# A mixture-of-experts kernel: the first search compares in three parts and is counted column by column, the first layer is cut at 256 tokens, and candidates are counted by a turning sum in all quarters

## The chip, the cores and the metric

The kernel runs on one core of a Trainium2 chip. The metric is the device time of one execution in microseconds, as the median of several runs. The core has engines that run side by side and wait for each other by semaphores: TensorE (PE in the profile; PEld are its weight loads), VectorE (DVE), ScalarE (ACT), GpSimd (POOL), and SyncE (SP), which here only issues transfers. VectorE's 128 lanes are the partitions; a quarter, or quadrant, is 32 of them.

## The reference

The program is an attention block followed by a layer of eight experts. Cut to what matters:

```python
kv = np.einsum('bhsd,bhse->bhde', k, v)                  # batch 8, heads 8, seq 576, head_dim 64
out = np.einsum('bhsd,bhde->bhse', q, kv)
rms = np.sqrt(np.mean(out * out, axis=-1, keepdims=True) + 1e-06)
x = (out / rms * g_norm)                                 # then reshaped to N = 4608 tokens of D = 512

cap = N // E                                             # 576 tokens for each of E = 8 experts
logits = x @ w_gate
for idx in np.argsort(-logits.flatten()):                # best pairs first
    tok, e = idx // E, idx % E
    if assigned[tok] >= 0 or counts[e] >= cap: continue
    assigned[tok] = e; counts[e] += 1
for e in range(E):                                       # w1: 512 x 1024, w2: 1024 x 512
    h = np.maximum(x[assigned == e] @ w1[e], 0.0)
    out[assigned == e] = h @ w2[e]
```

The greedy assignment fills the experts one after another. The kernel finds, for each round, the score at which the next expert becomes full, by a search over thresholds.

## The kernel before

**Attention** (to about 137 us) makes the tokens, writes them to `x_dram`, and leaves the logits in `lg`, laid out as 128 partitions by 36 columns (`GC`) for each expert. While it runs, `early` (line 280) already makes the first comparison of the first search for the columns that are ready.

**A search** is `threshold(t, over)` (line 493), for rounds t = 0 to 6. It has seven steps (`NSTEP`). In each step 32 candidate thresholds (`NCAND`) lie between two ends. `compare` (line 265) writes `over`: for each partition, column and candidate, whether the token's best score `mx` reaches the candidate, 36 x 32 = 1152 elements a partition. TensorE counts them by expert (line 503): nine matmuls, each with four columns of `over` (4 x 32 = 128) as weights and the same four columns of `best` as moving data. A product of 128 rows thus holds four column groups, of which only the blocks on the diagonal are wanted. VectorE subtracts three of these from `goal` (line 509, `need`), and compares the last with what remains (line 513, `full`; `n_full` counts the experts that are filled at a candidate). From the number of candidates with `n_full` above a half it derives the new ends.

For t = 0 that number is made by a matmul with ones (line 529, `k_ps`), and `pick_end` (line 521) reads the ends from a list. For t > 0 it is made on VectorE: line 543 spreads the flags in a 32 x 64 block, line 544 turns it in 32 x 32 blocks, line 545 sums it to `kk`, and line 549, once for each quarter of the partitions, multiplies `kk` by a width and adds the old lower end. Small values of these steps lie in one PSUM tile (`held_ps`), as named pieces.

After the seven steps, `assign` (line 560) settles which tokens the round takes and which expert it was; `fetch` (line 657) loads that expert's weights, works out the list of its tokens and gathers them from `x_dram` in five blocks of 128, the last of 64 (line 707, on GpSimd). `turn` (line 771) transposes each block on TensorE (line 783), and ScalarE copies it to `xt` with a factor (line 786). `warm` (line 652) gives TensorE matmuls without use[...].

**An expert's layers** are `layers(t)` (line 797). The first layer runs over two halves of the tokens, c = 0 and c = 1, of 288 columns each (`HALF`), and in each half over eight units of 128 hidden columns: four matmuls of 128 x 288 a unit (line 832; each appears as two records in the trace), then a ReLU on ScalarE (line 835). The second layer is a product of 2 x 2 blocks in seven multiplications instead of eight (line 881); block height is `TH` = 256 tokens, and GpSimd makes the sums of blocks (lines 813 and 823). The remaining 64 tokens follow at line 892.

**The order of the work** is written out by hand for TensorE, VectorE and ScalarE (`manual_schedule`, line 903). For the first expert, search, fetch and the turning of three of the five blocks are emitted first, then the first layer. From then on the layers of expert t are generated matmul by matmul, and each yields a cost. Searches for later rounds are a second generator that yields a due time: how much of TensorE's work is to lie before its next piece is emitted. A step of a search is due 4.6 us after the last one (line 498), the costs being 0.487 for a matmul of the first layer (line 834) and 0.38 for one of the second. So the count of a step stands in TensorE's queue behind about ten matmuls of a first layer, and in the meantime VectorE makes the next comparison. The blocks of the next expert's tokens are turned at places in the layers that yield `None`: two in the second layer (`turns`, line 873), one at line 896, and two inside the next first layer (the `yield 0` at line 837).

Of the kernel before, what the change touches and what calls it, by code (L numbers as in the profile page):

```python
# [7 lines left out]
FT = mybir.dt.float32  # L8
# [17 lines left out]
def kernel(  # L26
# [251 lines left out]
    over0 = asg.tile([P, GC, NCAND], BF, name="over", tag="over", bufs=2)  # L278

    def early(c0, c1):  # L280
        choose(c0, c1)
        compare(over0, cand0, c0, c1)
# [176 lines left out]
    for nm, shape in (("step", (2, NCAND + 3)), ("cut", (2, GC)), ("mx", (GC,)), ("code_mx", (GC,)), ("mine", (GC,)),  # L459
                      ("shut", (E,)), ("code", (E,)), ("some", (2 * QP,)), ("some_t", (2, QP + 1)),  # L460
# [18 lines left out]
    nc.vector.memset(small_ps["some_t"][0:QP, 0, QP:QP + 1], 1.0)  # L479
    nc.vector.memset(small_ps["some_t"][0:QP, 1, QP:QP + 1], 0.0)  # L480
# [12 lines left out]
    def threshold(t, over):  # L493
# [3 lines left out]
        for s in range(NSTEP):  # L497
            yield 4.6 if s > 0 else 0.4 if first else 2.0 if t == 1 else 2.4
# [3 lines left out]
            for c in range(0, GC, G):  # L502
                nc.tensor.matmul(n_ps, lhsT=over[:, c:c + G].rearrange("p c n -> p (c n)"),  # L503
                                 rhs=best[:, :, c:c + G],
                                 start=(c == 0), stop=(c == GC - G))
            need = goal[0:QP]
            for g in range(1, G):
# [7 lines left out]
            if s + 1 < NSTEP:  # L515
                over = asg.tile([P, GC, NCAND], BF, name="over", tag="over", bufs=2)
            if first:
# [13 lines left out]
                if s + 1 < NSTEP:  # L531
                    cand_next = small("cand", NCAND + 2)
                    compare(over, candidates(s + 1, lo, cand_next[:, 0:NCAND + 1]))
# [4 lines left out]
            else:  # L538
# [3 lines left out]
                some, some_t, kk = (small_ps[k][0:QP] for k in ("some", "some_t", "kk"))  # L542
                nc.vector.tensor_scalar(some, in0=n_full.to_broadcast([QP, 2 * QP]), scalar1=0.5, scalar2=None, op0=AL.is_gt)
                nc.vector.transpose(some_t[:, :, 0:QP], some.rearrange("p (t n) -> p t n", t=2))
                nc.vector.reduce_sum(out=kk, in_=some_t, axis=AXX)

                lo_was, (ends, cand_ps) = lo, pieces()
                for g in range(G):
                    nc.vector.tensor_scalar(ends[g * QP:(g + 1) * QP], in0=kk, scalar1=width[0:QP, s:s + 1],  # L549
                                            scalar2=lo_was[0:QP], op0=AL.mult, op1=AL.add)  # L550
# [202 lines left out]
    def control(t):  # L753
# [13 lines left out]
        if t + 1 < E - 1:  # L767
            compared[t + 1] = asg.tile([P, GC, NCAND], BF, name="over", tag="over", bufs=2)
            compare(compared[t + 1], candidates(0, bottom, pieces()[1]))

    def turn(t):
# [3 lines left out]
        if t == 0:  # L775
# [205 lines left out]
```

## Time and profile before

Three runs took 705.28, 705.42 and 708.66 us; the median is 705.42. The profiled execution has a span of 700.7 us.

| Stretch of the profile | us | TensorE busy | VectorE busy |
|---|---|---|---|
| attention | 0 to 137 | 88.93 | 77.58 |
| first search, before its result is used | 137 to 163 | 3.95 | 21.17 |
| assignment, list, weights, tokens, first turns | 163 to 179.2 | 9.62 | 13.54 |
| first expert | 179.2 to 244.9 | 65.44 | 52.48 |
| second to fifth expert | 244.9 to 506.8 | 260.37 | 219.06 |
| sixth expert | 506.8 to 568.8 | 62.00 | 13.72 |

A line of the timeline gives the start in us, the duration, the engine, the line of the kernel, the operation, what it writes and reads with the shapes (partitions x elements), how many instructions are merged, and in brackets how long the engine was idle before it and which instruction ended that. Matmul ends are modelled, so a busy TensorE is one that has matmuls in flight.

### The profile page before, as it was taken

The page shows a single profiled execution, that of the slowest core. Times are in us where ns is not written, and L with a number is a line of the kernel's source. Part 1 is how long each engine was busy: PE and PEld are TensorE (multiplying, and loading weights), DVE is VectorE, ACT ScalarE, POOL GpSimd, SP SyncE. Part 2 cuts the span into 40 slices and gives each one's busy share as a digit, 9 for nine tenths or more (in the row PEclk, how much of TensorE's full clock was granted, in tenths as well). Part 3 has the DMA queues.
Part 4 walks back from the last instruction along what each step waited for, and adds up shares of the span by engine and source line. Part 5 has one row for each costly group of instructions (what it writes and reads, how often), then busy time and mean ns, then how long its engine had stood idle before and what let it go on. Part 6 is the DMA issues. An engine that isn't in the chain of part 4 may idle for free.

```text
span 700.7 us, 13351 instructions
## 1 busy us (share of the span) xinstructions
PE 612.3 (87%) x5370; PEld 477.0 (68%) x5370; DVE 412.0 (59%) x1368; ACT 165.2 (24%) x355; POOL 288.7 (41%) x271
## 2 busy tenths in 40 slices
PE   3777686314999999999999999999999999999994
PEld 2566575211678677867786788678778867877782
DVE  4344666888678978888888888878650130010011
ACT  1454564710221122022102111211121022112100
POOL 0135433201263563535615651753284165426422
PEclk9998978555999999999999999999999999999997
DMA  8987797214501800810801610630371252010001
GB/s 284 320 288 262 256 347 284 92 46 144 164 1 51 301 25 3 306 60 8 307 2 68 246 64 15 232 130 1 107 252 59 79 187 69 1 54 14 0 1 67
DMA packets 41405, 91.05 MB, mean 130 GB/s; under 512 B 3456, under 2 KB 3456, under 8 KB 41344
## 3 DMA queue, kind: packets, MB, share of 16 engines
q1 hardware_dynamic: 34752, 71.31, 29.1%
q0 software_dynamic: 5888, 18.88, 7.8%
q8 instruction: 42, 0.69, 0.4%
q14 instruction: 19, 0.16, 0.1%
q10 hardware_dynamic: 704, 0.02, 0.1%
HBM read 71.32 MB, written 18.87 MB: 129 GB/s over the span
## 4 chain that ended last, share of the span: by engine, by line
PE 79%; DVE 10%; issue 4%; DMA 2%; ACT 2%; POOL 1%; POOLq 0%; ACTq 0%; DVEq 0%; SPq 0%
PE h_ps L832 34%; PE y_ps L881 27%; PE y_ps L892 4%; PE o_ps L372 3%; PE qt_ps L301 3%; PE t_ps L783 3%; PE kv_ps L313 2%; PE given_ps L503 2%; DVE over L266 1%; DMA gw<-in_moe_w_gate_dram 1%; DVE kv L321 1%; DMA w_sb<-in_moe_w_dram 1%; DVE ms L380 1%; PE w_ps L340 1%; ACT sq L378 1%
## 5 line engine op out<-in xcount | busy, mean ns | idle before, releaser
L832 PE MATMUL h_ps<-xt,w_sb 128*128 128x288 f32 x1024 | 261.8, 410 | 0.8 <-ACT xt L786 0.8
L832 PEld LDWEIGHTS h_ps<-xt,w_sb 128*128 128x128 f32 x1024 | 189.8, 190 | 54.9 <-issue 5.7
L835 ACT ACTIVATE hid<-h_ps 128x288 f32<-128x288 f32 x128 | 52.5, 410 | 207.0 <-PE h_ps L832 197.9
L881 PE MATMUL y_ps<-tw,sh 128*128 128x256 f32 x384 | 87.3, 381 | 0.0
L852 DVE TENSOR_TENSOR y_sb<-y_ps,u 128x512 f32<-128x512 f32 x24 | 16.5, 689 | 113.8 <-PE y_ps L881 113.3
L881 PEld LDWEIGHTS y_ps<-tw,sh 128*128 128x128 f32 x384 | 71.7, 190 | 9.1
L823 POOL TENSOR_TENSOR sh<-hid 128x512 f32<-128x512 f32 x32 | 40.6, 1268 | 86.4 <-ACT hid L835 86.4
L707 POOL DMA_INDIRECT xg<-x_dram,ids x40 | 38.1, 953 | 68.5 <-DMA w_sb<-in_moe_w_dram 42.7
L786 ACT ACTIVATE xt<-t_ps,g_col 128x512 f32<-128x512 f32 (+1 forms) x40 | 25.8, 644 | 144.9 <-PE t_ps L783 112.0
L881 PE MATMUL y_ps<-w_sb,hid 128*128 128x256 f32 x256 | 58.3, 382 | 0.0
L266 DVE TENSOR_TENSOR over<-mx,held_ps 128x1152 bf16<-128x1152 f32 x42 | 56.8, 1353 | 1.5
L881 PEld LDWEIGHTS y_ps<-w_sb,hid 128*128 128x128 f32 x256 | 48.0, 190 | 6.6
L859 POOL TENSOR_TENSOR y_sb<-u,u 128x512 f32<-128x512 f32 x8 | 10.2, 1270 | 96.2 <-DVE u L852 96.2
L399 POOL TENSOR_TENSOR xo<-o_sb,inv 128x512 f32<-128x512 f32 x31 | 32.5, 1078 | 34.6 <-ACT sq L378 17.3
L790 POOL DMA_INDIRECT out_dram<-y_sb,outs x32 | 31.3, 977 | 37.1 <-issue 21.2
L813 POOL TENSOR_TENSOR tw<-w_sb 128x512 f32<-128x512 f32 x32 | 39.9, 1269 | 12.1 <-DMA w_sb<-in_moe_w_dram 11.9
L549 DVE TENSOR_SCALAR held_ps<-held_ps,width 32x2 f32<-32x2 f32 x144 | 41.3, 287 | 5.3
L503 PEld LDWEIGHTS <-over 128*128 128x128 bf16 x441 | 17.6, 97 | 38.2 <-DVE over L266 27.3
L372 PE MATMUL o_ps<-kvx,qt 64*64 64x72 f32 x1152 | 31.0, 251 | 9.5 <-issue 8.8
L503 PE MATMUL given_ps<-best,over 128*128 128x32 bf16 x441 | 19.3, 179 | 21.4 <-DVE over L266 19.2
L372 PEld LDWEIGHTS o_ps<-kvx,qt 64*64 64x64 f32 x1152 | 25.3, 153 | 15.1 <-issue 13.6
L380 DVE TENSOR_REDUCE ms<-sq 128x8 f32<-128x512 f32 x36 | 24.0, 679 | 17.9 <-ACT sq L378 17.8
(210 smaller groups left out, 827.4 us busy)
## 6 DMA issues: line engine op xcount, KB each, us to landing
w_sb<-in_moe_w_dram SPq DMA_DIRECT2D x16, 1024.0 KB, 6.8
w_sb<-in_moe_w_dram SPq DMA_DIRECT2D x8, 2048.0 KB, 15.7
k_sb<-in_k_dram SPq DMA_DIRECT2D x16, 576.0 KB, 5.5
v_sb<-in_v_dram SPq DMA_DIRECT2D x16, 576.0 KB, 5.9
q_sb<-in_q_dram SPq DMA_DIRECT2D x16, 576.0 KB, 5.0
x_dram<-xo SPq DMA_DIRECT2D x16, 512.0 KB, 4.3
x_dram<-xo SPq DMA_DIRECT2D x4, 256.0 KB, 4.2
xg<-x_dram,ids POOLq DMA_INDIRECT x40
```

Source lines behind the costliest of these rows:

```text
L266: nc.vector.tensor_tensor(over[:, c0:c1], mx[:, c0:c1].rearrange("p (c o) -> p c o", o=1).to_broadcast([P, c1 - c0, NCAND]), cand[:, 1:NCA ...
L372: nc.tensor.matmul(o_ps[n * HP:(n + 1) * HP, rp, (2 * r2 + l) * W:(2 * r2 + l + 1) * W], lhsT=turned_q[bn][ks, block // 2, l * HP:(l + 1) ...
L399: nc.gpsimd.tensor_tensor(xo[:, t], o_sb[:, t, :, 0:D], inv[:, t * H:(t + 1) * H].rearrange("p (h o) -> p h o", o=1).to_broadcast([P, H, D ...
L503: nc.tensor.matmul(n_ps, lhsT=over[:, c:c + G].rearrange("p c n -> p (c n)"), rhs=best[:, :, c:c + G], start=(c == 0), stop=(c == GC - G))
L549: nc.vector.tensor_scalar(ends[g * QP:(g + 1) * QP], in0=kk, scalar1=width[0:QP, s:s + 1], scalar2=lo_was[0:QP], op0=AL.mult, op1=AL.add)
L707: tokens = nc.gpsimd.indirect_dma_start(out=xg[0:nr], out_offset=None, in_=x_dram, in_offset=bass.IndirectOffsetOnAxis(ap=ids[0:nr, n:n + ...
L790: put = nc.gpsimd.indirect_dma_start(out=out, out_offset=bass.IndirectOffsetOnAxis(ap=ids_of[t][0:nr, n:n + 1], axis=0), in_=y_sb[0:nr, :] ...
L813: in_order(nc.gpsimd.tensor_tensor(o[:, m:m + 2], x[:, m:m + 2], y[:, m:m + 2], op=AL.subtract))
L823: in_order(nc.gpsimd.tensor_tensor(o[:, ms], x[:, ms], y[:, ms], op=op))
L832: nc.tensor.matmul(h_ps, lhsT=w1[:, 2 * (d % 2) + d // 2, f * P:(f + 1) * P], rhs=xt[:, d, cs], start=(d == 0), stop=(d == DC - 1))
L835: nc.scalar.activation(hid[:, f, cs], h_ps, ACT.Relu)
L881: nc.tensor.matmul(p_ps[:, n], lhsT=left[:, f, n * P:(n + 1) * P], rhs=right[:, f], start=(f == 0), stop=(f == FH - 1))
```

## The change

Three things are done. **First**, in the search of round 0 the comparison is cut into three instructions of 12 columns each, written to three tiles, so that TensorE can begin to count while VectorE still compares; and TensorE counts each column by itself (36 matmuls with 32 columns of weights), which leaves one sum for each candidate and no subtractions. **Second**, the first layer's tokens are divided at 256 instead of 288, so the first part needs two blocks of tokens and not three; three blocks instead of two are then turned inside the first layer, and one place in the second layer goes. **Third**, in later rounds the spread of the flags is written into all four quarters, with a constant (`one_more`) added that makes one of the two sums larger by one; a reduction that transposes its input as it reads (`apply_transpose`) gives `kk` on all 128 partitions, and one instruction makes the ends in place of four. The due time of these steps goes from 4.6 to 4.2. Beside that, `over` of the later rounds moves to another memory pool.

```diff
--- before.py
+++ after.py
@@ -275,11 +275,20 @@
     cand0 = small("cand", NCAND + 2)
     candidates(0, bottom, cand0[:, 0:NCAND + 1])
     nc.vector.tensor_copy(cand0[:, NCAND + 1:NCAND + 2], top)
-    over0 = asg.tile([P, GC, NCAND], BF, name="over", tag="over", bufs=2)
+    THIRD = GC // 3
+    over0 = [asg.tile([P, THIRD, NCAND], BF, name="over_c", tag=f"over{n}", bufs=2) for n in range(3)]
+
+    def compare_thirds(over, cand, c0=0, c1=GC):
+        for n in range(3):
+            a, b = max(c0, n * THIRD), min(c1, (n + 1) * THIRD)
+            if a < b:
+                nc.vector.tensor_tensor(
+                    over[n][:, a - n * THIRD:b - n * THIRD], mx[:, a:b].rearrange("p (c o) -> p c o", o=1).to_broadcast([P, b - a, NCAND]),
+                    cand[:, 1:NCAND + 1].rearrange("p (o n) -> p o n", o=1).to_broadcast([P, b - a, NCAND]), op=AL.is_ge)
 
     def early(c0, c1):
         choose(c0, c1)
-        compare(over0, cand0, c0, c1)
+        compare_thirds(over0, cand0, c0, c1)
 
 
 
@@ -457,7 +466,7 @@
     held = psm.tile([P, 512], FT, name="held_ps", tag="s", bufs=1)
     at = 0
     for nm, shape in (("step", (2, NCAND + 3)), ("cut", (2, GC)), ("mx", (GC,)), ("code_mx", (GC,)), ("mine", (GC,)),
-                      ("shut", (E,)), ("code", (E,)), ("some", (2 * QP,)), ("some_t", (2, QP + 1)),
+                      ("shut", (E,)), ("code", (E,)), ("some", (2 * QP,)), 
                       ("kk", (2,)), ("which", (1,)), ("over_room", (E,)), ("last", (E,)), ("half", (NB,)),
                       ("rise", (2, GC))):
         n = shape[0] * (shape[1] if len(shape) > 1 else 1)
@@ -476,8 +485,10 @@
             small_ps[nm] = small_ps[nm].rearrange("p (t n) -> p t n", t=shape[0])
         at += n
     nc.vector.tensor_copy(small_ps["rise"], rise)
-    nc.vector.memset(small_ps["some_t"][0:QP, 0, QP:QP + 1], 1.0)
-    nc.vector.memset(small_ps["some_t"][0:QP, 1, QP:QP + 1], 0.0)
+
+    one_more = asg.tile([QP, 2 * QP], FT, name="one_more")
+    nc.vector.memset(one_more[:, 0:QP], 1.0 / QP)
+    nc.vector.memset(one_more[:, QP:2 * QP], 0.0)
     turn_of = [0]
 
     def pieces():
@@ -495,16 +506,22 @@
         lo, hi = bottom, top
         first, cand = t == 0, cand0
         for s in range(NSTEP):
-            yield 4.6 if s > 0 else 0.4 if first else 2.0 if t == 1 else 2.4
+            yield (4.6 if t == 0 else 4.2) if s > 0 else 0.4 if first else 2.0 if t == 1 else 2.4
 
 
             n_ps = small_ps["n"]
-            for c in range(0, GC, G):
-                nc.tensor.matmul(n_ps, lhsT=over[:, c:c + G].rearrange("p c n -> p (c n)"),
-                                 rhs=best[:, :, c:c + G],
-                                 start=(c == 0), stop=(c == GC - G))
+            if first:
+
+                for c in range(GC):
+                    nc.tensor.matmul(n_ps[0:QP, :, 0], lhsT=over[c // THIRD][:, c % THIRD], rhs=best[:, :, c],
+                                     start=(c == 0), stop=(c == GC - 1))
+            else:
+                for c in range(0, GC, G):
+                    nc.tensor.matmul(n_ps, lhsT=over[:, c:c + G].rearrange("p c n -> p (c n)"),
+                                     rhs=best[:, :, c:c + G],
+                                     start=(c == 0), stop=(c == GC - G))
             need = goal[0:QP]
-            for g in range(1, G):
+            for g in range(1, 1 if first else G):
                 less = small("need", E)[0:QP]
                 nc.vector.tensor_tensor(less, need, n_ps[g * QP:(g + 1) * QP, :, g], op=AL.subtract)
                 need = less
@@ -513,7 +530,8 @@
             nc.vector.scalar_tensor_tensor(full, in0=n_ps[0:QP, :, 0], scalar=0.0, in1=need, op0=AL.add,
                                            op1=AL.is_ge, accum_out=n_full)
             if s + 1 < NSTEP:
-                over = asg.tile([P, GC, NCAND], BF, name="over", tag="over", bufs=2)
+                over = moe.tile([P, GC, NCAND], BF, name="over", tag="over", bufs=2) if not first else [
+                    asg.tile([P, THIRD, NCAND], BF, name="over_c", tag=f"over{n}", bufs=2) for n in range(3)]
             if first:
                 ends = small("ends", 2)
                 hi, lo = ends[:, 0:1], ends[:, 1:2]
@@ -530,7 +548,7 @@
                 pick_end(0)
                 if s + 1 < NSTEP:
                     cand_next = small("cand", NCAND + 2)
-                    compare(over, candidates(s + 1, lo, cand_next[:, 0:NCAND + 1]))
+                    compare_thirds(over, candidates(s + 1, lo, cand_next[:, 0:NCAND + 1]))
                 pick_end(1)
                 if s + 1 < NSTEP:
                     nc.vector.tensor_copy(cand_next[:, NCAND + 1:NCAND + 2], hi)
@@ -539,15 +557,14 @@
 
 
 
-                some, some_t, kk = (small_ps[k][0:QP] for k in ("some", "some_t", "kk"))
-                nc.vector.tensor_scalar(some, in0=n_full.to_broadcast([QP, 2 * QP]), scalar1=0.5, scalar2=None, op0=AL.is_gt)
-                nc.vector.transpose(some_t[:, :, 0:QP], some.rearrange("p (t n) -> p t n", t=2))
-                nc.vector.reduce_sum(out=kk, in_=some_t, axis=AXX)
+                some, kk = small_ps["some"], small_ps["kk"]
+                for g in range(G):
+                    nc.vector.scalar_tensor_tensor(some[g * QP:(g + 1) * QP], in0=n_full.to_broadcast([QP, 2 * QP]), scalar=0.5,
+                                                   in1=one_more, op0=AL.is_gt, op1=AL.add)
+                nc.vector.tensor_reduce(kk, some.rearrange("p (t n) -> p t n", t=2), axis=AXX, op=AL.add, apply_transpose=True)
 
                 lo_was, (ends, cand_ps) = lo, pieces()
-                for g in range(G):
-                    nc.vector.tensor_scalar(ends[g * QP:(g + 1) * QP], in0=kk, scalar1=width[0:QP, s:s + 1],
-                                            scalar2=lo_was[0:QP], op0=AL.mult, op1=AL.add)
+                nc.vector.tensor_scalar(ends, in0=kk, scalar1=width[:, s:s + 1], scalar2=lo_was, op0=AL.mult, op1=AL.add)
                 lo = ends[:, 1:2]
                 if s + 1 < NSTEP:
                     compare(over, candidates(s + 1, lo, cand_ps))
@@ -765,16 +782,13 @@
                 yield None
         yield None if t == 0 else 0.5
         if t + 1 < E - 1:
-            compared[t + 1] = asg.tile([P, GC, NCAND], BF, name="over", tag="over", bufs=2)
+            compared[t + 1] = moe.tile([P, GC, NCAND], BF, name="over", tag="over", bufs=2)
             compare(compared[t + 1], candidates(0, bottom, pieces()[1]))
 
     def turn(t):
 
         xt = moe.tile([P, DC, CAP], FT, name="xt", tag="xt", bufs=1)
         turned[t] = xt
-        if t == 0:
-            yield
-            yield
         for n, (a, nr) in enumerate(blocks):
             xg = rows_of.pop((t, n))
             tag = "y" if t == 0 and n % 2 else "t"
@@ -825,15 +839,16 @@
 
         units = [k * FH + f for f in range(FH) for k in range(2)]
         for c, f in [(c, f) for c in range(2) for f in units]:
-            cs = slice(c * HALF, (c + 1) * HALF)
-            h_ps = psm.tile([P, HALF], FT, name="h_ps", tag="h")
+            cs = slice(0, TH) if c == 0 else slice(TH, CAP)
+            n_c = cs.stop - cs.start
+            h_ps = psm.tile([P, n_c], FT, name="h_ps", tag="h")
             for d in range(DC):
 
                 nc.tensor.matmul(h_ps, lhsT=w1[:, 2 * (d % 2) + d // 2, f * P:(f + 1) * P], rhs=xt[:, d, cs],
                                  start=(d == 0), stop=(d == DC - 1))
-                yield 0.487
+                yield 0.487 * n_c / HALF
             nc.scalar.activation(hid[:, f, cs], h_ps, ACT.Relu)
-            if c == 0 and f in units[1:4:2]:
+            if c == 0 and f in units[1:6:2]:
                 yield 0
             if c == 1 and f in units[3::4]:
                 sums(f % FH - 1)
@@ -870,7 +885,7 @@
                 put(t, n, P, y_of[0][:, n])
 
 
-        turns = {(6, 2), (6, 6)} if t == 0 else {(5, 6), (6, 3)}
+        turns = {(6, 6)} if t == 0 else {(6, 3)}
         for m, (left, right, then) in enumerate(
                 ((a11, b11, lambda p_ps: nc.scalar.copy(u1, p_ps)), (a12, b21, first_c),
                  (a22, t4, lambda p_ps: nc.scalar.copy(u5, p_ps)), (s2, t2, lambda p_ps: add(u2, p_ps, u1)),
@@ -905,11 +920,11 @@
         while next(ctl) is not None:
             pass
         first = turn(0)
-
-        for _ in range(1 + (HALF + P - 1) // P):
+        for _ in ctl:
+            pass
+
+        for _ in range(2):
             next(first)
-            next(ctl, None)
-        next(first)
 
 
         searches = ((n, what) for n in range(1, E) for what in control(n))
```

## The prediction

> **What bounds the kernel now.** I read the shares of the page first, then busy time in windows cut where a stage ends (the columns are start and end, length, busy time of PE, PEld, DVE, ACT and POOL, TensorE clock, DMA), then the timeline inside two of these.
>
> ```profile
> PE 612.3 (87%) x5370; PEld 477.0 (68%) x5370; DVE 412.0 (59%) x1368; ACT 165.2 (24%) x355; POOL 288.7 (41%) x271
> ...
> 137.00:163.00 26.00, 3.95 (x66) 2.90 (x67) 21.17 (x95) 6.09 (x26) 0.00 (x0) 0.50 0.13 52
> 163.00:179.20 16.20, 9.62 (x44) 4.12 (x42) 13.54 (x47) 2.06 (x3) 4.91 (x5) 0.64 0.61 202
> 179.20:244.90 65.70, 65.44 (x369) 50.52 (x369) 52.48 (x184) 10.93 (x23) 29.30 (x26) 1.00 0.35 124
> 506.80:568.80 62.00, 62.00 (x284) 48.49 (x285) 13.72 (x42) 11.53 (x25) 30.64 (x27) 1.00 0.38 133
> ```
>
> There are three regimes. To 137 us is attention, which the edits hardly touch. From 137 to 179 us TensorE is nearly idle: the first search (seven steps) runs as a serial chain of VectorE and TensorE, then tokens and weights are fetched. From 179 us TensorE is the bound: in the first expert's 65.7 us it is busy 65.44. An expert without a search beside it takes 62.0 us; the difference is mostly the search's own matmuls. So VectorE time saved in a later search is worth nothing by itself; a microsecond off the stretch 137 to 179 us is worth one.
>
> One step of the first search:
>
> ```profile
> 139.03 1.36 DVE L266 TENSOR_TENSOR over<-mx,cand 128x1152 bf16<-128x1152 f32 x1
> 140.30 0.25 DVE L523 SCALAR_TENSOR_TENSOR at<-row_f,k_ps,cand 128x33 f32<-128x33 f32 x1
> ...
> 140.44 0.42 PE L503 MATMUL given_ps<-best,over 128*128 128x32 bf16 x9 [2.03 <-DVE over L266]
> ...
> 140.90 0.15 DVE L509 TENSOR_TENSOR need<-goal,given_ps 32x8 f32<-32x8 f32 x1
> 141.09 0.36 DVE L509 TENSOR_TENSOR need<-need,given_ps 32x8 f32<-32x8 f32 x2
> 141.48 0.15 DVE L513 SCALAR_TENSOR_TENSOR full<-given_ps,need 32x8 f32<-32x8 f32 x1
> ```
>
> The compare (1.36 us) ends at 140.39, nine count matmuls follow at once, then three subtractions fold four column groups, then `full`. From compare to compare a step is 3.62 us (139.03 to 142.65), nothing hidden.
>
> A step of a later search, VectorE only:
>
> ```profile
> 199.41 0.21 DVE L543 TENSOR_SCALAR held_ps<-n_full 32x64 f32<-32x64 f32 x1
> 199.66 0.25 DVE L544 STREAM_TRANSPOSE held_ps<-held_ps 32x64 f32<-32x64 f32 x1
> 199.95 0.22 DVE L545 TENSOR_REDUCE held_ps<-held_ps 32x2 f32<-32x66 f32 x1
> 200.21 1.26 DVE L549 TENSOR_SCALAR held_ps<-held_ps,width 32x2 f32<-32x2 f32 x4
> 201.50 0.26 DVE L271 TENSOR_SCALAR held_ps<-away,held_ps 128x33 f32<-128x33 f32 x1
> ```
>
> The stretch that the change rewrites, L543 to L271, is 2.09 us. The start of the first layer:
>
> ```profile
> 176.94 0.69 ACT L786 ACTIVATE xt<-t_ps,g_col 128x512 f32<-128x512 f32 x1 [0.44 <-PE t_ps L783]
> ...
> 178.44 0.69 ACT L786 ACTIVATE xt<-t_ps,g_col 128x512 f32<-128x512 f32 x1 [0.81 <-PE t_ps L783]
> ...
> 179.18 2.69 PE L832 MATMUL h_ps<-xt,w_sb 128*128 128x288 f32 x10 [0.78 <-ACT xt L786]
> ```
>
> It waits for the third block of tokens (ready 179.13), since 288 tokens need three; the second is ready at 177.63.
>
> [...] the four L549 writes, one per quadrant, take 1.26 us in a row at 0.29 each, while L594 and L596, independent and in the same quadrant, start 0.07 us apart at 0.16 each, and L523 above starts 0.09 us before the compare ends. [...] No row of before loads 32 bf16 columns; the count's 128-column loads follow each other every 0.026 us. [...] L544 (64 elements, turned) 0.25 us, L543 (64, not turned) 0.21.
>
> **The change, part by part.**
>
> *First search.* A third is 384 elements a partition. Between the rows of L266 at 256 (0.416 us) and 512 (0.680) lies 0.548. [...] each starts 0.09 us before the last one ends: starts at 0, 0.46, 0.92, end at 1.47 instead of 1.36. TensorE gets 36 matmuls instead of 9; the first 24 lie beside the second and third compare. Their pitch I take as the 0.026 us of the nine ((0.42 - 0.21) / 8, a lone one being 0.21), so twelve take 0.31 us a third, under the 0.46 in which the next third comes. After the last third: 0.05 to start, 11 x 0.026 + 0.21 = 0.50, 0.04 to VectorE: `full` starts at 2.06 us after the compare began; before it was 141.48 - 139.03 = 2.45, the 0.58 us of subtractions included. Gain 0.39 a step, six times 2.34. The first step's compare is done before: it loses the subtractions (0.58) and gets three more matmuls (0.08), 0.50. Sum **2.8 us**, all on the path: the expert's index, its weights, ids and tokens follow from it. The pitch is the unknown: lower bound 0.026[...]. I take the lower since L585 to L588, with 8 moving columns like the new ones, start 0.03 us apart.
>
> *First layer at 256.* Columns 256 + 320 = 2 x 288. The pitch is 0.216 us at 256 (20.29/94 of L881) and 0.245 at 288 (23.48/96 of L832), so proportional, and above the weight load's 0.190: no cost. The layer needs two blocks, so the first expert starts at 177.68 instead of 179.18: 1.50. But the third block's transposes, until now in the gap, enter the layer at 0.44 us (as 249.28 on the chain): **1.06 net**. Its tokens are there at 177.77 (its transposes start then), its slot comes 8 matmuls after the start, so no wait. The weights' two halves run at about 400 GB/s from 167.5 to 174 us, ahead of 177.7, and move with the index. For later experts one block's turn moves from the second layer into the first, 0.44 us in either: zero. In the first expert the block at product 6, place 2 had waited for its tokens (0.27 idle, then 0.66 instead of 0.44); at place 6 it does not: **0.49**.
>
> *Turning sum.* Removed: L543, L544, L545 and three of the L549, 2.09 us with the last. Added: four scalar_tensor_tensor of 64 elements[...], about 0.22 + 0.03 each (L543's size): 1.00; the turned sum, 0.25 as L544, with its gap 0.29; one L549 0.32. Together 1.61, gain 0.48 a step. If they overlapped it would be 0.85; if the new forms cost half more, about 0. The due time falls from 4.6 to 4.2 with it. In the first layer that means a count each 10 matmuls of 0.432 or 8 of 0.546, with the count itself (0.27) 4.59 to 4.64 us; before, 10 of 0.489 and 5.16. From the count's start to the end of the next compare VectorE needs 0.42 + 4.50 = 4.92 now, 4.44 then: slack 0.24 before, 0.15 to 0.20 after. A count that comes late holds the layer's matmuls queued behind it. I take zero for this part; its worth is only what TensorE waits now, under 2 us in all searches.
>
> *The rest* (memory of `over`, the constants, the order of the last search parts and the first turns, early compares cut at 12 and 24 columns) lies under attention or beside waits: zero.
>
> Sum: 2.8 + 1.06 + 0.49 = 4.4 us. 705.4 - 4.4 = **701.0**.
>
> **Rivals.**
> *The narrow count is slow*[...] For it: no row with 32-column loads. Against: the 0.03 us of L585 to L588.
> *The later searches hold TensorE.* If the four writes and the turned sum cost as much as what they replace, VectorE's 4.92 meets a period of 4.6 less the 0.24 that the loads need ahead: 0.5 us late in about 18 steps (36 later steps, half of them beside a first layer), +9: 705.4 - 4.4 + 9 = 710. For it: the margin is thin[...]. Against: four 0.29 us writes go.
> *The earlier start is hidden*, by weights or by a wait inside the layer: only 2.8 and a little: 702.4. For it: first weights land within 4 us of the start. Against: they move with the search.
> *Waits fall*: the writes overlap, and the half us waits on `since` and `over` go: 2 us more, 699.
>
> **Chances.** Forecast 0.57, slow count 0.08, later searches hold 0.08, hidden start 0.15, waits fall 0.12. Range 698.5 to 705.2: from the last rival past the hidden start with part of a stall; the two slower rivals lie outside. Faster by over 0.5% (below 701.9): most of the forecast and all of "waits fall", with a little of the hidden start: 0.60; slower than 708.9: 0.07; the rest 0.33.
>
> **What would show it.** First search: 3.23 us from step to step, three compares of 0.55 us, no L509 there, the twelve last matmuls 0.5 us. First layer's first matmul 1.5 us nearer to the tokens (4.3 earlier in all, near 174.9). Later steps: 1.6 us from the first of four writes to L271. Experts 0 to 4 still 65 to 66 us. I am wrong if the count's pitch is over 0.04 us, if TensorE shows idle time before counts beyond 2 us in sum, or if the turned sum takes over 0.4 us.

## The result, and the profile after

The changed kernel takes **737.79 us** (median of four runs, 734.94 to 740.78) against 706.58 for the kernel before (four runs, 705.28 to 708.66). The ratio is 1.044, with a 95% interval of 1.039 to 1.049: some 31 us slower. The forecast was 701.0.

The page of the changed kernel: the shares of the engines, the chain that ended last, and the group of the new instruction (busy us, mean ns of one, idle time before).

```profile
PE 629.5 (86%) x5559; PEld 489.8 (67%) x5559; DVE 434.0 (59%) x1318; ACT 165.5 (22%) x355; POOL 288.5 (39%) x271
...
PE 69%; DVE 22%; issue 4%; ACT 2%; DMA 1%; POOL 0%; POOLq 0%; SPq 0%; DVEq 0%; ACTq 0%
...
L562 DVE SCALAR_TENSOR_TENSOR held_ps<-n_full,one_more 32x64 f32<-32x64 f32 x168 | 77.7, 462 | 5.8
```

VectorE has 50 instructions fewer than before and is busy 22 us longer, and it holds 22% of the chain that ended last (10% before). The last line says where: the 168 quarter writes of the turning sum have a mean of 462 ns, twice the 0.22 us that the forecast gave them.

Windows cut at the stages (start and end, length, busy time of PE, PEld, DVE, ACT and POOL, TensorE clock, DMA): the first three experts and an expert without a search.

```profile
177.00:247.70 70.70, 65.77 (x377) 50.38 (x377) 58.06 (x184) 10.96 (x23) 29.03 (x26) 1.00 0.33 118
247.70:326.60 78.90, 67.99 (x370) 52.05 (x368) 69.00 (x193) 11.54 (x24) 29.43 (x26) 0.94 0.24 84
326.60:403.90 77.30, 67.58 (x375) 51.88 (x373) 68.20 (x202) 11.54 (x24) 30.57 (x27) 0.96 0.23 82
...
541.50:603.40 61.90, 61.90 (x285) 48.47 (x283) 13.70 (x42) 11.54 (x24) 30.61 (x27) 1.00 0.32 106
```

The expert without a search is as long as before (61.9 us; 62.0 before). The first expert, 65.7 us before, takes 70.7 with TensorE busy 65.77 of it: 4.9 us of idle time that was 0.3. The second takes 78.9. All the loss lies in experts that have a search beside them; the five that follow each other from 177 us take 70.8, 78.9, 77.2, 69.7 and 68.0 us, together 364.5 where they took 327.5 before.

The first search, in which the change works as meant. One step, from its three compares to the next three (start, length, engine, line; in brackets, idle time and what ended it):

```profile
140.50 1.50 DVE L285 TENSOR_TENSOR over_c<-mx,cand 128x384 bf16<-128x384 f32 x3
...
141.11 1.43 PE L516 MATMUL given_ps<-best,over_c 128*32 128x8 bf16 x36 [1.23 <-DVE over_c L285]
...
142.58 0.15 DVE L530 SCALAR_TENSOR_TENSOR full<-given_ps,goal 32x8 f32<-32x8 f32 x1 [0.22 <-PE given_ps L516]
...
143.75 1.50 DVE L285 TENSOR_TENSOR over_c<-mx,cand 128x384 bf16<-128x384 f32 x3
```

The 36 narrow counts begin while the second compare runs, no subtraction stands between them and `full`, and a step is 3.25 us (143.75 - 140.50) where it was 3.62. And the start of the first layer:

```profile
176.22 0.69 ACT L800 ACTIVATE xt<-t_ps,g_col 128x512 f32<-128x512 f32 x1 [0.52 <-PE t_ps L797]
...
176.96 1.35 PE L847 MATMUL h_ps<-xt,w_sb 128*128 128x256 f32 x5
```

The layer starts 0.05 us after the second block of tokens is ready (176.91). Before, it started at 179.18, behind the third.

The later searches. First a step in which nothing is held, then the next one, beside GpSimd's weight differences (L827):

```profile
185.48 1.02 DVE L562 SCALAR_TENSOR_TENSOR held_ps<-n_full,one_more 32x64 f32<-32x64 f32 x4
186.53 0.27 DVE L564 TRANSPOSE_TENSOR_REDUCE held_ps<-held_ps 128x2 f32<-128x64 f32 x1
186.83 0.29 DVE L567 TENSOR_SCALAR held_ps<-held_ps,width 128x2 f32<-128x2 f32 x1
187.16 0.26 DVE L271 TENSOR_SCALAR held_ps<-away,held_ps 128x33 f32<-128x33 f32 x1
...
191.13 4.38 DVE L562 SCALAR_TENSOR_TENSOR held_ps<-n_full,one_more 32x64 f32<-32x64 f32 x4
191.71 2.48 POOL L827 TENSOR_TENSOR tw<-w_sb,tw 128x512 f32<-128x512 f32 x2
194.15 2.48 POOL L827 TENSOR_TENSOR tw<-w_sb 128x512 f32<-128x512 f32 x2
195.55 0.27 DVE L564 TRANSPOSE_TENSOR_REDUCE held_ps<-held_ps 128x2 f32<-128x64 f32 x1
...
197.88 0.39 PE L520 MATMUL given_ps<-best,over 128*128 128x32 bf16 x9 [2.83 <-DVE over L266]
```

Up to 187.16 all is as forecast: four writes in 1.02 us, 1.68 us from the first to L271. Six microseconds later the same four writes take 4.38 us. Taken one by one they end at 191.84, 193.06, 194.29 and 195.51, and GpSimd's instructions end at 191.75, 192.97, 194.19 and 195.41: each write ends 0.08 to 0.10 us after one of them. The last line shows the price: TensorE stands for 2.83 us before its count. The longest case is in the second expert:

```profile
252.13 0.91 POOL L804 DMA_INDIRECT out_dram<-y_rest,outs  x1 [3.75 <-DVE need L526]
...
252.66 11.09 DVE L562 SCALAR_TENSOR_TENSOR held_ps<-n_full,one_more 32x64 f32<-32x64 f32 x4
253.06 2.50 POOL L827 TENSOR_TENSOR tw<-w_sb 128x512 f32<-128x512 f32 x2
...
266.12 0.42 PE L520 MATMUL given_ps<-best,over 128*128 128x32 bf16 x9 [9.20 <-DVE over L266]
```

Here the first of the four writes takes 10.30 us, through a whole row of eight GpSimd instructions (253.06 to 262.87 us), and TensorE waits 9.20 us. The write began 0.40 us before the row, under a scatter of output rows (L804), and at the median of 231 ns it would have been over when the row began. The source view of L562 (durations least/median/most in ns, first and last start) and TensorE's waits for VectorE in the searches sum it up (total us, times, longest):

```profile
L562 DVE SCALAR_TENSOR_TENSOR held_ps<-n_full,one_more x168: 220/231/10297, 180.4 to 520.9; 32x64 f32<-32x64 f32 x168
```

```profile
PE given_ps L520 <- DVE over L266: 25.3, 11, 9.2
PE given_ps L602 <- DVE sums L595: 6.7, 1, 6.7
```

The median write is 231 ns. Of 168 writes 30 were over 0.3 us, in 14 of 42 steps; what they take above 231 ns each is 39.2 us in sum. TensorE's two waits are 32.0 us. The same trace, taken write by write, says beside what they are held: 27 began while a GpSimd difference or sum was running, and all 27 were held; 31 began under one of GpSimd's gathers or scatters, and 29 of these took 0.24 us at most, while the other two (10.30 and 1.96 us) ran on into a difference or sum that followed within 0.03 us; of the other 110 only one took over 0.24 us (0.31).

**Theory.** The new write reads two operands from SBUF (`n_full` and `one_more`); the L543 that it replaces read one. The theory is that a VectorE instruction with two SBUF inputs does not go on while GpSimd forms differences or sums from SBUF. The ends above agree (0.08 to 0.10 us after GpSimd's), and the 27 of 27. The 29 writes beside gathers and scatters (0.24 us at most) say that not all of GpSimd's work counts. **Rivals:** the new form or its order is slow beside any work (four writes in four quarters and a turned sum); the shorter due time of 4.2 asks too much of VectorE; or the narrow counts and the 256-token division cost something after all.

### The profile page after: what moved, and what is told of

Its sections match the earlier page's. It is cut to its first block, busy times and chain, and to the rows that moved or that the text cites. A ratio compares the mean times of both kernels' runs of the same rounds, so it can differ in the third digit from the quotient of the medians.

```text
span 735.9 us, 13683 instructions
## 1 busy us (share of the span) xinstructions
PE 629.5 (86%) x5559; PEld 489.8 (67%) x5559; DVE 434.0 (59%) x1318; ACT 165.5 (22%) x355; POOL 288.5 (39%) x271
## 4 chain that ended last, share of the span: by engine, by line
PE 69%; DVE 22%; issue 4%; ACT 2%; DMA 1%; POOL 0%; POOLq 0%; SPq 0%; DVEq 0%; ACTq 0%
PE h_ps L847 29%; PE y_ps L896 21%; DVE held_ps L562 8%; DVE over L266 3%; PE y_ps L907 3%; PE qt_ps L310 3%; PE o_ps L381 3%; PE t_ps L797 2%; PE kv_ps L322 2%; DMA v_sb<-in_v_dram 1%; PE given_ps L520 1%; PE given_ps L516 1%; DVE need L526 1%; PE warm_ps L672 1%; PE w_ps L349 1%
## 5 line engine op out<-in xcount | busy, mean ns | idle before, releaser
L847 PE MATMUL h_ps<-xt,w_sb 128*128 128x320 f32 (+1 forms) x1024 | 269.2, 417 | 0.1
L847 PEld LDWEIGHTS h_ps<-xt,w_sb 128*128 128x128 f32 x1024 | 192.8, 194 | 55.8 <-issue 6.7
L850 ACT ACTIVATE hid<-h_ps 128x320 f32<-128x320 f32 (+1 forms) x128 | 52.5, 410 | 230.0 <-PE h_ps L847 224.5
L896 PE MATMUL y_ps<-tw,sh 128*128 128x256 f32 x384 | 85.8, 381 | 0.0
L837 POOL TENSOR_TENSOR sh<-hid 128x512 f32<-128x512 f32 x32 | 40.5, 1265 | 105.3 <-ACT hid L850 105.2
L562 DVE SCALAR_TENSOR_TENSOR held_ps<-n_full,one_more 32x64 f32<-32x64 f32 x168 | 77.7, 462 | 5.8
L266 DVE TENSOR_TENSOR over<-mx,held_ps 128x1152 bf16<-128x1152 f32 x42 | 56.9, 1354 | 1.6 <-DVE held_ps L271 0.2
L874 POOL TENSOR_TENSOR y_sb<-u,u 128x512 f32<-128x512 f32 x8 | 10.1, 1266 | 99.8 <-DVE u L867 99.8
L804 POOL DMA_INDIRECT out_dram<-y_sb,outs x32 | 31.3, 977 | 40.7 <-issue 29.2
L827 POOL TENSOR_TENSOR tw<-w_sb 128x512 f32<-128x512 f32 x32 | 39.9, 1268 | 12.8 <-DMA w_sb<-in_moe_w_dram 12.6
L381 PE MATMUL o_ps<-kvx,qt 64*64 64x72 f32 x1152 | 32.5, 258 | 9.8 <-issue 8.8
L520 PEld LDWEIGHTS <-over 128*128 128x128 bf16 x378 | 14.2, 96 | 37.2 <-DVE over L266 33.7
L520 PE MATMUL given_ps<-best,over 128*128 128x32 bf16 x378 | 16.2, 177 | 25.3 <-DVE over L266 25.3
```

The source lines that it names most:

```text
L266: nc.vector.tensor_tensor(over[:, c0:c1], mx[:, c0:c1].rearrange("p (c o) -> p c o", o=1).to_broadcast([P, c1 - c0, NCAND]), cand[:, 1:NCA ...
L381: nc.tensor.matmul(o_ps[n * HP:(n + 1) * HP, rp, (2 * r2 + l) * W:(2 * r2 + l + 1) * W], lhsT=turned_q[bn][ks, block // 2, l * HP:(l + 1) ...
L562: nc.vector.scalar_tensor_tensor(some[g * QP:(g + 1) * QP], in0=n_full.to_broadcast([QP, 2 * QP]), scalar=0.5, in1=one_more, op0=AL.is_gt, ...
L804: put = nc.gpsimd.indirect_dma_start(out=out, out_offset=bass.IndirectOffsetOnAxis(ap=ids_of[t][0:nr, n:n + 1], axis=0), in_=y_sb[0:nr, :] ...
L827: in_order(nc.gpsimd.tensor_tensor(o[:, m:m + 2], x[:, m:m + 2], y[:, m:m + 2], op=AL.subtract))
L837: in_order(nc.gpsimd.tensor_tensor(o[:, ms], x[:, ms], y[:, ms], op=op))
```

## The experiments

Times are medians; ratios are to the kernel before, with their 95% interval. It was timed again beside each of three series: 706.32 us beside the first four experiments, 706.23 beside the four from the second series (sum_only_psum, pool_fills, psum_again, first_search_only), 706.02 beside the other four. A gain in us on the kernel before is taken from the ratio, which need not be that of the medians.

### The constant in PSUM, and the old sum

one_more_psum is the changed kernel with the constant moved:

```diff
-    one_more = asg.tile([QP, 2 * QP], FT, name="one_more")
+    one_more = small_ps["one_more"][0:QP]
```

> The changed kernel with one edit: the constant added to the flags lies in PSUM and not in SBUF, so the four writes of the flags read one operand from SBUF and one from PSUM. Theory A (a VectorE instruction with two SBUF inputs waits for GpSimd's running sums): the four writes fall from a mean of 0.46 us to 0.22 to 0.23, TensorE's waits for counts go, and the time falls by some 35 us to 699 to 704 us, below the kernel before. Theory B (what holds them is the write into four quarters of one PSUM tile, or the turning sum): the mean stays at 0.46 us and the time at 735 to 738. Theory C (the due time of 4.2 us is too early): no difference either.

Measured: 697.94 us, 0.987 (0.979 to 0.995). The same instructions in the same order, due time and divisions as in the changed kernel are 40 us faster when one operand lies elsewhere. This takes away the rivals of the form, the due time and the first two parts at once.

old_sum keeps parts one and two and puts the old sum of before (L543 to L549 there, due time 4.6) back:

> The changed kernel with its third part undone: flags, turn, sum and four ends as before, due time 4.6; the comparison in thirds and the division at 256 stay. Theory A and B: 701 to 703 us, 3 to 5 us under the kernel before (first search 2.8 to 3.3, first layer about 1). Rival D (the first two parts cost something too, through the transposes moved into the first layer): at or above 705.

Measured: 700.33 us, 0.994 (0.991 to 0.997): 4.2 us (2.5 to 6.1) faster than before, where the forecast's first two parts had been worth 4.4. Its first expert takes 65.1 us, an expert without search 62.0.

### The turning sum alone

sum_only is the kernel before with part three and nothing else:

> The kernel before with the third part alone (flags into four quarters with the constant in SBUF, turning sum, one ends, due 4.2). Theory A and B: 738 to 743 us, all of the loss and none of the gain. Rival D: clearly under the changed kernel's 738.

Measured: 761.21 us, 1.078 (1.068 to 1.088), 55 us slower than before and well outside what was expected. The source view of its writes:

```profile
L546 DVE SCALAR_TENSOR_TENSOR held_ps<-n_full,one_more x168: 220/231/10303, 186.3 to 545.4; 32x64 f32<-32x64 f32 x168
```

The median is the same 231 ns; 32 writes were held, 47.2 us in sum, two of them through whole rows (10.30 and 9.80 us). So part three alone carries the loss, but its size was not the 31 us of the changed kernel plus the 4 of the other parts: it depends on which steps meet GpSimd's rows.

due_46 tests that: the changed kernel, only with the old due time.

```diff
-            yield (4.6 if t == 0 else 4.2) if s > 0 else 0.4 if first else 2.0 if t == 1 else 2.4
+            yield 4.6 if s > 0 else 0.4 if first else 2.0 if t == 1 else 2.4
```

> The changed kernel with the due time of a later step back at 4.6. Theory A: the writes wait for GpSimd as before, and the counts come later in TensorE's queue by one matmul, so at most a few us better: 730 to 738 us. Theory C (counts are due too early for a chain that is only a little longer): back to 700 to 705.

Measured: 749.88 us, 1.062 (1.052 to 1.072), outside both expectations: longer due times made it slower, not faster.

```profile
L562 DVE SCALAR_TENSOR_TENSOR held_ps<-n_full,one_more x168: 220/231/10294, 184.0 to 535.8; 32x64 f32<-32x64 f32 x168
```

Only 24 writes were held here, but three of them through rows of 9.8 to 10.3 us, 48.0 us in sum. The number of held writes does not set the loss; the rows do. The pace of the search changes which writes meet them, in either direction, and the rival that 4.2 us asks too much falls.

sum_only_psum is sum_only with the constant in PSUM:

> The kernel before with the third part alone, the constant in PSUM. Theory A (the loss is the second SBUF input): no loss left, 703 to 707 us, 55 us under the same part with the constant in SBUF. The step of a later search is 0.45 to 0.5 us shorter on VectorE, but TensorE has other work there, so within 2 us of the kernel before. Rival (the early due times cost something of their own): 708 or more.

Measured: 707.27 us, 1.002 (1.000 to 1.004). 54 us less than sum_only, by the place of one operand. Its step beside a first layer is 4.68 us against 5.16 before, and the kernel gains nothing by it.

### Both ends of the meeting

If the second SBUF input is the cause, moving the other operand must help as well, and so must a GpSimd that doesn't read. n_full_psum leaves the constant in SBUF and moves `n_full`:

```diff
-            n_full = small("n_full")[0:QP]
+            n_full = small("n_full")[0:QP] if first else small_ps["n_full"][0:QP]
```

> The changed kernel with the constant left in SBUF and the other operand, the counts of filled experts, in PSUM. Theory A (it is the number of SBUF inputs that counts, not which one): as with the constant in PSUM, all writes near 0.23 us, 697 to 702 us. Rival (something about the constant's tile or its address): writes of 1.2 us and 10 us stay, over 730 us.

Measured: 701.66 us, 0.990 (0.984 to 0.996).

```profile
L562 DVE SCALAR_TENSOR_TENSOR held_ps<-held_ps,one_more x168: 220/228/235, 181.6 to 484.4; 32x64 f32<-32x64 f32 x168
```

No write is over 235 ns. Either operand will do, so it is the pair, not this constant or its address.

pool_fills is the changed kernel with both operands in SBUF as they were; GpSimd's differences and sums in L827 and L837 become fills of the same tiles, which write SBUF and read nothing. The differences and sums are left out of the computation.

```diff
-                in_order(nc.gpsimd.tensor_tensor(o[:, m:m + 2], x[:, m:m + 2], y[:, m:m + 2], op=AL.subtract))
+                in_order(nc.gpsimd.memset(o[:, m:m + 2], 0.001))
...
-                in_order(nc.gpsimd.tensor_tensor(o[:, ms], x[:, ms], y[:, ms], op=op))
+                in_order(nc.gpsimd.memset(o[:, ms], 0.001))
```

> The changed kernel, its constant in SBUF as it was, but GpSimd's differences and sums of blocks (two tiles) are left out: it fills the same tiles with a constant and so reads nothing from SBUF there. Theory A in the form that only GpSimd's reads matter: the four writes are at 0.23 us in nearly every case and the time is 695 to 703 us. If any GpSimd work held VectorE, writes too: writes of 0.5 us and more remain beside the fills. Theory B (four quarters): 0.46 us on the mean as before and over 730 us.

Measured: 702.34 us, 0.995 (0.992 to 0.997). The writes, and one of the two groups of fills:

```profile
L562 DVE SCALAR_TENSOR_TENSOR held_ps<-n_full,one_more x168: 220/231/687, 181.4 to 484.7; 32x64 f32<-32x64 f32 x168
...
L837 POOL MEMSET sh<- x64: 535/542/552, 181.2 to 638.8; 128x512 f32 x64
```

Two of 168 writes are long, 0.62 us in sum, and both lie beside GpSimd's output sums (L874), which still read SBUF. A fill is also shorter (0.54 us) than a difference (1.22 us from start to start), but 25 writes began while a fill was running, and none of them took over 236 ns; in the changed kernel all 27 that began under a difference or sum were held. So the writes wait for something that differences and sums do and fills don't. Reading tensors from SBUF is what the edit took away; the fill is also another operation, so whether it is the reading or the operation is not shown.

### Fewer writes with two SBUF inputs

one_of_four lets only the first quarter's write read the constant from SBUF; the other three read a copy in PSUM.

```diff
-                                                   in1=one_more, op0=AL.is_gt, op1=AL.add)
+                                                   in1=one_more if g == 0 else in_psum, op0=AL.is_gt, op1=AL.add)
```

> The changed kernel; of the four writes only the first reads the constant from SBUF, the other three from PSUM. Theory A in its detail (each of four writes in a row waits for the next GpSimd instruction, so the dose counts): the runs of 1.2 us go, the long waits of 8 to 10 us behind eight instructions stay where the first write meets them; the loss is a third or less: 702 to 715 us. If one wait a step is enough to lose everything: 730 or more.

Measured: 727.28 us, 1.028 (1.022 to 1.035), between the two expectations. The group of the 42 writes that still read SBUF, from its page:

```profile
L564 DVE SCALAR_TENSOR_TENSOR held_ps<-n_full,one_more 32x64 f32<-32x64 f32 x42 | 31.1, 741 | 1.4
```

Thirteen of the 42 are held, 21.7 us in sum, and two rows (10.30 and 7.67 us) make 17.5 of it. The short holds of 1.2 us, one after the other, are gone; a row needs only one write to be caught. With three quarters of the exposed writes removed, 20 of the 31 us lost were still lost.

### The same cause without the turning sum

cand_sbuf is the kernel before; only the candidates of the later searches lie in SBUF, so that the compare L266 reads two SBUF operands (the edit is shown for one of its two places; the first compare of a search is changed alike).

```diff
-                    compare(over, candidates(s + 1, lo, cand_ps))
+                    compare(over, candidates(s + 1, lo, small("cand_sb", NCAND + 1)))
```

> The kernel before with another instruction given two SBUF inputs: the candidates of the later searches lie in SBUF, so the compare of 128 x 1152 reads scores and candidates from there. Theory A as a rule for any VectorE instruction: compares that meet GpSimd's differences and sums take 1.36 us and up to the rest of a GpSimd instruction or of a row of them more, and the time rises, to 715 to 740 us. Rival (only writes into another quarter are held): compares stay at 1.36 us and the time at 704 to 708.

Measured: 726.13 us, 1.026 (1.019 to 1.034): about as slow as expected, but for the most part in another instruction. The source views of the two lines:

```profile
L266 DVE TENSOR_TENSOR over<-mx,cand_sb x42: 1357/1359/2373, 179.1 to 513.8; 128x1152 bf16<-128x1152 f32 x42
```

```profile
L271 DVE TENSOR_SCALAR cand_sb<-away,held_ps x36: 247/248/8172, 187.1 to 513.6; 128x33 f32<-128x33 f32 x36
```

Five compares are long, 5.05 us in sum. L271, which reads one SBUF tensor and a PSUM scalar and now writes SBUF, is held in 10 of these 36 cases, 20.1 us in sum, up to 8.17. In the kernel before the same instruction wrote PSUM; 11 of its 36 began while a GpSimd difference or sum was running, and none took over 261 ns. The place of its output is all that changed in it; why that place counts, no run shows. Counting SBUF inputs alone would have missed this one. The timeline shows the reverse as well:

```profile
193.77 3.60 POOL L813 TENSOR_TENSOR tw<-w_sb,tw 128x512 f32<-128x512 f32 x2
193.88 2.37 DVE L266 TENSOR_TENSOR over<-mx,cand_sb 128x1152 bf16<-128x1152 f32 x1
```

A compare of 1.36 us takes 2.37, and the two GpSimd instructions beside it 3.60 instead of 2.48: the first ran as always (1.26 us), the second was held by the compare (2.38 us).

### The best version, and what its parts are worth

psum_again is one_more_psum a second time, beside two parts of it.

> The changed kernel with the constant in PSUM, timed a second time and in more rounds, beside its third part alone. If the third part brings something once it no longer waits for GpSimd, this is 1 us or more under the first two parts alone (which gained 4 us on the kernel before); if TensorE hides it, it equals them, 700 to 703 us.

Measured: 698.98 us, 0.991 (0.989 to 0.993): 6.3 us faster than before, and the fastest version. Its writes, and TensorE's waits for VectorE in the searches:

```profile
L562 DVE SCALAR_TENSOR_TENSOR held_ps<-n_full,held_ps x168: 216/224/231, 183.8 to 485.6; 32x64 f32<-32x64 f32 x168
```

```profile
PE given_ps L520 <- DVE over L266: 1.4, 1, 1.4
```

No write is over 231 ns, and the 32.0 us of waits are 1.4. The first five experts as one window, of the changed kernel and of this one:

```profile
176.96:541.49 364.53, 332.51 (x1817) 254.91 (x1817) 296.75 (x896) 57.10 (x119) 152.24 (x134) 0.97 0.29 102
```

```profile
180.30:506.23 325.93, 324.54 (x1817) 251.52 (x1818) 256.60 (x896) 57.11 (x119) 152.32 (x134) 1.00 0.33 115
```

They take 38.6 us less. TensorE is idle for 32.0 us of the first and 1.4 of the second, which makes 30.6; the other 8.0 are matmuls that take longer (332.5 us busy for the same number). In the changed kernel the granted clock falls to 0.5 three times in this stretch, for 20.4 us in all, the first time from 261.4 to 271.6 us, in the wait of 9.20 us and behind it, where the matmuls of 128 x 256 start every 0.427 us instead of every 0.216; in psum_again it stays at 1.00. That the 39.2 us of held writes are so near to the 38.6 us lost is chance: some 9 us of the holding did not reach TensorE as waits, and the lower clock took 8.

first_search_only keeps part one and takes parts two and three away:

> The kernel before with the first part alone (thirds, count column by column). The prediction's term: 2.8 us under the kernel before, all of it between the end of attention and the first expert's index. If the first layer's division brings what was predicted (1.06 + 0.49), this is 1.5 us slower than both parts together.

Measured: 704.11 us, 0.997 (0.995 to 0.999), so a gain of 2.3 us (0.6 to 3.8) for part one, 1.9 less than parts one and two together; 1.5 less was expected, and the intervals overlap.

psum_due_46 is the best version with the old due time of 4.6:

> The changed kernel with the constant in PSUM and the due time back at 4.6. If the shorter step is worth anything, it comes through the earlier counts: then this is 1 to 2 us slower than with 4.2, near the first two parts alone (4 us under the kernel before). If the due time is idle: the same as with 4.2, 6 us under.

Measured: 702.02 us, 0.993 (0.989 to 0.996). 5.2 us of gain instead of 6.3, with overlapping intervals: a step beside a first layer is 5.16 us instead of 4.62, and the time hardly shows it. The instructions of a step are the same in both, so there its length is set by the due time, not by VectorE's chain.

## Why the prediction was wrong, point by point

**Right: the first search.** Gain a step 0.37 us (3.62 to 3.25) for 0.39; `full` 2.08 us after the compares begin (142.58 - 140.50) for 2.06; the narrow counts follow each other every 0.027 us for 0.026, so that the rival "the narrow count is slow" falls; three compares in 1.50 us for 1.47. The first step gained 0.51 for 0.50. Part one alone measured 2.3 us for 2.8, inside its interval.

**Right: the first layer at 256.** From the last `full` of the first search to the first layer 18.12 us instead of 19.59: 1.47 for 1.50. The division costs nothing (61.9 and 62.0 us for an expert without search). Parts one and two together measured 4.2 us for 4.4. The absolute time of the start, 176.96, is not the 174.9 named: 2.0 of these 2.1 us lie in the attention, whose end differs between the two profiled executions (the last of the early compares starts at 136.69 and at 138.68). The weights came at 370 GB/s (before, 168 to 174 us), not at about 400, and were not waited for.

**Right only where nothing meets it: the turning sum.** Four writes 1.02 us for 1.00, the turned sum 0.265 for 0.25, the chain from the first write to L271 1.68 for 1.61. That the four follow each other without overlap (0.26 us from start to start) is not shown to come from their quarters, nor is that shown for the four L549 that the prediction cites: in the traces each of the four waits for a semaphore that VectorE raises at the end of the one before. A step beside a first layer in which nothing is held takes 4.62 us, as the prediction's sum of the due times has it (4.59 to 4.64), instead of 5.16.

**Failed: the price of the four writes.** The forecast put each of the four at "about 0.22 + 0.03 each (L543's size)", 1.00 in all. L543 has the same shape, but one SBUF input; the new write has two. In the median it does cost 0.231 us; in the mean 0.462, and one set of four took 11.09 us. From this the next sentence, "I take zero for this part", failed: the part cost some 35 us instead (the 31 lost and the 4 that the other parts bring). The forecast bounded the writes by overlap from below and by "half more" from above; work of another engine was in neither bound. The sign of being wrong that it named, TensorE idle before counts for more than 2 us in sum, came true with 32.0 us.

The profile of before had such waits in it, in the attention, where GpSimd multiplies tokens from SBUF (L399) beside VectorE:

```profile
109.70 5.21 POOL L399 TENSOR_TENSOR xo<-o_sb,inv 128x512 f32<-128x512 f32 x5 [4.75 <-ACT o_sb L379]
...
112.29 0.69 DVE L252 TENSOR_TENSOR pick<-lg,mx 128x64 f32<-128x64 f32 x1
113.02 0.97 DVE L253 TENSOR_TENSOR pick<-pick,code 128x64 f32<-128x64 f32 x1
114.02 0.26 DVE L255 TENSOR_REDUCE code_mx<-pick 128x8 f32<-128x64 f32 x1
```

L252 and L253 have two SBUF inputs. At 130.7 and 130.9 us, with no GpSimd instruction beside them, the same two take 0.22 us each; here they take 0.69 and 0.97, and each ends 0.08 us after one of the five of L399. The reduction L255, with one SBUF input, starts beside them and is not held: 0.26 us, as at 131.2 us with nothing beside it.

How often the new writes would be caught could then have been estimated. GpSimd's 17 differences and sums of an expert at 1.24 us are 21 us of 65, or 32%; in psum_again 54 of the 168 writes, 32%, began while one was running. Taken as one instant a step, that is 13 or 14 of 42 steps; 14 were hit. So close a match owes something to luck, as four writes stand in line for 1.0 us and a held step moves those behind it. What could not have been had is the size of a hit, 2.8 us in the mean (39.2 / 14), as rows count far more than single instructions.

**The rival on the other side** ("the later searches hold TensorE", 710 us) named the place and not the reason: it made 18 steps 0.5 us late each, where 28 of the 42 steps are on time and 14 lose 2.8 us each. Its direction was right, its size was a seventh of the loss.

**Zero for a shorter step was right.** sum_only_psum, the shorter step alone, is at 1.002 (1.000 to 1.004). On top of the other two parts it may be worth 2 us (6.3 against 4.2), but the two intervals overlap, so this is not shown.

## What to carry to other kernels

Price an added VectorE instruction by a row with the same places of its operands and its output, not only the same form and size: here two inputs in SBUF cost next to nothing by themselves (0.231 us against 0.224 with one in PSUM), and up to a whole row of another engine's work (10.30 us) while GpSimd added or subtracted from SBUF. Look in the profile for one instruction of the same shape with two durations. The share of time that GpSimd spends on such work in that stage gives an estimate of how often it will happen; the slack of whoever waits for VectorE gives whether it counts. Where the instruction can't be moved, keep one operand in PSUM: here one line was worth 39 to 40 us.

## What the runs showed that was not expected

A write with two SBUF inputs sometimes gets in after one GpSimd instruction (1.2 us) and sometimes waits for all of a row (10.30 us over eight, 7.64 over seven). Over the five slow kernels the traces divide cleanly. All 12 instructions that were caught in the weight differences (L827) of the second or a later expert waited to the end of the row; those rows begin 0.02 to 0.03 us after a scatter of GpSimd. All 16 that were caught in the first expert's row, which begins after 11 us or more of idle GpSimd, were let in after one instruction. Which of these differences decides stays open: no run changes what stands in front of a row.

The holding goes both ways (a compare of 2.37 us, and a GpSimd difference of 2.38 instead of 1.22 beside it), and it reaches a tensor_scalar from SBUF to SBUF with a scalar in PSUM (8.17 us instead of 0.25).

An accumulator read into PSUM instead of SBUF took 129 ns instead of 71 (n_full_psum), which with 42 steps is 2.4 us of VectorE's time.

Here a long wait cost more than its length. The granted clock went to 0.5 some 4.5 us into the wait of 9.20 us and 4 us into one of 6.7 us, and stayed there for 10.2 and 6.8 us, so that the matmuls behind the wait ran on at the lower clock. Over the first five experts of the changed kernel the mean clock was 0.97; in the kernel before and in psum_again it was 1.00.
